# Storing dK and dV from ACT's queue in one transfer of 2 MB, instead of from GpSimd's in two

## The chip, the cores and the metric

One core of a Trainium2 chip. The time is the device time in microseconds (us) of one execution of the whole kernel; the kernel before took 701.58 us, the median of three runs (698.41 to 702.56). Engines: PE is TensorE, DVE is VectorE, ACT is ScalarE, POOL is GpSimd, SP is SyncE. Transfers (DMAs) between HBM and the core's SBUF are issued by an engine's queue and then carried out by 16 channels (DMA engines), which all queues share.

## What is computed

The backward pass of an attention with grouped heads (32 query heads, 4 key/value heads, 4 query positions, 2048 keys, 128 features, 32 batches, bfloat16), with the forward output as well:

```python
B, Hq, Hkv, Sq, Sk, D = 32, 32, 4, 4, 2048, 128
def _fwd_reference(q, k, v):
    k = jnp.repeat(k, rep, axis=1)
    v = jnp.repeat(v, rep, axis=1)
    scores = jnp.einsum("bhqd,bhkd->bhqk", q, k) * D ** -0.5
    p = _softmax(scores, axis=-1)
    return jnp.einsum("bhqk,bhkd->bhqd", p, v)
_out, _vjp = jax.vjp(_f, q, k, v)
return (out, *vjp(grad_out))        # O, dQ, dK, dV
```

K, V, dK and dV are 2.1 MB each for one batch; Q, dO, O and dQ are 32 KB each.

## The kernel before

One batch is one unit of work. The 32 query rows of each of the four K/V heads stand side by side on 128 partitions (`G` = 32 rows a head). For each batch the steps are, by their names in the kernel:

- `LK`, `LV` (lines 145 to 160): four loads of 512 KB each for K and for V, one a head, issued by SP. K has 3 buffers, V has 2. A load waits until its buffer's last reader is done: dQ for K, O for V. `LK` of the next batch but one also brings, every fourth batch, Q and dO of four batches (`GROUP`, line 137; POOL issues it).
- `QDT`, `KT0..7`, `VT0..7` (lines 167 to 190): PE turns Q, dO, K and V by multiplying with the identity matrix, DVE copies the result from PSUM to SBUF.
- `Sa`, `Sb` (line 206): scores on PE, row maximum on DVE (`negb`). `EXa`, `EXb` (line 215): Exp on ACT.
- `NRM` (line 234): 1/sum on DVE (`rinv`), then POOL makes `dop` = dO/sum and `qp` = scaled Q/sum, four instructions each (line 231). PE needs `dop` for dV and `qp` for dK.
- `ET`, `O` (lines 253, 270): E turned, the output O, and delta; POOL stores O. `dPa`, `dPb` (line 334): the gradient `ds` of the scores. `dST`, `dQ` (lines 256, 284): `ds` turned, and dQ; POOL stores dQ.
- `dV0..7`, `dK0..7` (lines 328 to 332, by `outer`, line 292): eight outer products each. PE writes two PSUM banks, and ACT casts them (line 307, 128 x 1024 elements) into a 2 MB tile in SBUF. There are 4 such tiles for dV and dK together (`out_pool`), so the tile of a batch's dK is that of dK two batches earlier, and its first cast waits until the earlier store has landed. After the eighth cast the tile is stored: `left` counts them (lines 314 to 326). The last batch is stored in four halves instead, by POOL (line 319), as they become ready.

PSUM has 8 banks, handed out by a small planner in the program (`Banks`) by age; PE waits when the bank that it was given has not yet been read by ACT or DVE.

The order of the work is written out by hand: `HEAD` for the first batches, `STEADY`, which is repeated, and `TAIL`. The instructions of each engine stand in its queue in that order, and each engine works its queue in order. In `STEADY` (`-` is the batch before, `+` the one after, `+2` the one after that) the places that matter are:

```python
dSTa- VT4 EXa VT0 QDT+ dSTb- KT4+ dK1- dK6- KT6+ KT2+ KT0+ NRM dK0- dQ- dK3- dK5- dK2- ETb ETa VT7 KT3+ VT6 VT1
dV7 dK4- O dV5 dPb dV1 KT5+ KT1+ dV3 dV6 dPa KT7+ dV2 LK+2 LV+2 VT2+ dV4 Sa+ dV0 Sb+ dK7 VT5+ VT3+ EXb+
```

`dK4-` is the eighth dK of its batch and `dV0` the eighth dV, so dK's store is issued behind `dK4-` and dV's behind `dV0`. Behind them stand, for ACT, the casts of `dV5` and of `dK7`, and the Exps.

Of the kernel before, what the change touches and what calls it, by code (L numbers as in the profile page):

```python
# [81 lines left out]
def kernel(ctx: ExitStack, tc: tile.TileContext, q, k, v, grad_out, out_0, out_1, out_2, out_3):  # L82
    nc = tc.nc
# [48 lines left out]
    store = nc.gpsimd  # L132
# [159 lines left out]
    def outer(S, x, y, dst, name, i, b, copy):  # L292

        if name not in S:
            S[name + "left"] = 8
            S[name] = out_pool.tile([P, NH, C, D], BF16, name=name, tag="outp")
        t = banks.take(2)
        ps = banks.ap(t).rearrange("p a (j c d) -> p a j c d", j=2, c=2)
        for c in range(2):
            u = P * ((2 * i + c) % 8)  # L300
            for a in range(2):
                r = slice(2 * G * a, 2 * G * a + 2 * G)
                nc.tensor.matmul(  # L303
                    ps[:, a, :, c, :], lhsT=S[f"{x}{i // 4}"][r, u:u + P], rhs=S[y][r, :, :],
                    start=True, stop=True, tile_position=(2 * G * a, 0),
                )
        copy(  # L307
            out=S[name][:, :, 2 * i:2 * i + 2, :].rearrange("p h c d -> p h (c d)"),
            in_=banks.ap(t).rearrange("p a (j w) -> p (a j) w", j=2),
        )  # L310
        banks.give(t)
        S[name + "left"] -= 1
        if b == B - 1:

            half = f"{name}half{i // 4}"
            S[half] = S.get(half, 4) - 1
            if S[half] == 0:
                c = slice(8 * (i // 4), 8 * (i // 4) + 8)
                store.dma_start(
                    out=dst[b].rearrange("p h (c d) -> p h c d", d=D)[:, :, c, :].rearrange("p h c d -> p h (c d)"),  # L320
                    in_=S[name][:, :, c, :].rearrange("p h c d -> p h (c d)"),
                )
        elif S[name + "left"] == 0:
            o = S.pop(name)
            for a in range(2):
                store.dma_start(out=dst[b][:, 2 * a:2 * a + 2, :], in_=o[:, 2 * a:2 * a + 2].rearrange("p h c d -> p h (c d)"))  # L326

    def dV(b, i, copy=nc.scalar.copy):
        outer(st[b], "e", "dop", dv_v, "dv", i, b, copy)

    def dK(b, i, copy=nc.scalar.copy):
        outer(st[b], "ds", "qp", dk_v, "dk", i, b, copy)
# [29 lines left out]
    with tc.manual_schedule():  # L362

        for w in HEAD.split():
            w, b = w.split("@")
# [5 lines left out]
        for w in TAIL.split():  # L371
            w, b = w.split("@")
# [31 lines left out]
```

## The time and the profile before

| | us |
|---|---|
| median of three runs | 701.58 (698.41 to 702.56) |
| the profiled execution | 698.71 |
| its span, first to last instruction | 696.7 |
| PE busy / ACT busy / DVE busy / POOL busy | 626.0 / 569.1 / 584.5 / 302.7 |
| moved by transfers | 274.44 MB, mean 394 GB/s |

The profile is of one execution. A page gives the busy time of each engine, the span in 40 slices (busy share in tenths; GB/s is what the transfers moved in the slice), the costliest groups of instructions and the DMA issues with the median time from issue to landing. A row of the list of waits reads "engine line waited for: us in total, times, longest us": `ACT dk L307 <- DMA out_dram<-dk: 7.1, 8, 1.8` is ACT idle before the cast at line 307 until a store of dK had landed, eight times, 7.1 us in all. A row of a timeline reads start, length, engine, line and operation, output and input, count, and in brackets the idle time before it and what ended it; instructions of one kind in a row are merged. "issue" is the call that puts a transfer into a queue; its length is not that of the transfer.

### The profile page before, as it was taken

The numbers are of one execution on the slowest core, as the hardware profiler recorded it, in microseconds if no ns is written. First come the engines' busy times: TensorE is split into PE (matmuls) and PEld (weight loads), VectorE is DVE, ScalarE is ACT, GpSimd is POOL, SyncE is SP. The second block draws the span as 40 slices with busy tenths as digits, with TensorE's granted clock in tenths as the row PEclk, the third lists the DMA queues.
The fourth block names the chain that finished last, engine by engine and source line by source line (L and its number), as shares of the span: only waits on it lengthen the run. The fifth ranks groups of instructions, "written<-read, shape, count | busy, mean of one in ns | idle before, by whom it ended". The sixth has DMA issues, their size and how long they took to land.

```text
span 696.7 us, 28064 instructions
## 1 busy us (share of the span) xinstructions
PE 626.0 (90%) x12352; PEld 454.1 (65%) x12352; DVE 584.5 (84%) x992; ACT 569.1 (82%) x673; POOL 302.7 (43%) x506
## 2 busy tenths in 40 slices
PE   5899999999998989979999798998998889998982
PEld 4577776677676656666666676667766677666661
DVE  5999999999997998869988688888988869898960
ACT  0698989899887989869888687887888868888994
POOL 1355443555454435443354424544434543345452
PEclk9999999999999999999999899999999989999997
DMA  9989999999999999999999999999999999999767
GB/s 339 400 317 411 417 415 416 416 413 415 417 415 417 414 417 416 417 409 412 415 415 413 373 397 398 400 410 382 416 416 417 415 340 393 415 414 415 289 257 274
DMA packets 75577, 274.44 MB, mean 394 GB/s; under 512 B 8448, under 2 KB 8448, under 8 KB 75456
## 3 DMA queue, kind: packets, MB, share of 16 engines
q0 software_dynamic: 37536, 138.16, 49.3%
q1 hardware_dynamic: 37920, 134.50, 48.9%
q8 instruction: 96, 1.57, 0.8%
q14 instruction: 25, 0.20, 0.1%
HBM read 136.31 MB, written 136.31 MB: 391 GB/s over the span
## 4 chain that ended last, share of the span: by engine, by line
PE 43%; DMA 33%; ACT 6%; DVE 5%; POOL 5%; issue 5%; SPq 0%; POOLq 0%; DVEq 0%; ACTq 0%
PE banks L181 18%; DMA k_sb<-in_k_dram 15%; DMA out_dram<-dk 12%; PE banks L303 10%; PE banks L264 7%; ACT dv L307 5%; PE banks L248 5%; DMA out_dram<-dv 4%; PE banks L198 3%; POOL dop L231 2%; DMA v_sb<-in_v_dram 2%; DVE kt L183 2%; DVE ds L338 1%; ACT dk L307 1%; POOL qp L231 1%
## 5 line engine op out<-in xcount | busy, mean ns | idle before, releaser
L307 ACT CAST dv<-banks 128x1024 bf16<-128x1024 f32 x256 | 245.5, 1028 | 56.9 <-PE banks L303 56.3
L307 ACT CAST dk<-banks 128x1024 bf16<-128x1024 f32 x256 | 250.7, 1025 | 34.5 <-PE banks L303 23.6
L183 DVE COPY kt<-banks 128x1024 bf16<-128x1024 bf16 x256 | 164.3, 680 | 8.3 <-PE banks L181 8.3
L183 DVE COPY vt<-banks 128x1024 bf16<-128x1024 bf16 x256 | 166.2, 680 | 1.3 <-PE banks L181 0.9
L181 PE MATMUL banks<-ident,k_sb 128*128 128x128 bf16 x2048 | 145.8, 221 | 13.1 <-DMA k_sb<-in_k_dram 8.6
L181 PE MATMUL banks<-ident,v_sb 128*128 128x128 bf16 x2048 | 143.5, 220 | 14.3 <-ACT dv L307 9.7
L231 POOL TENSOR_SCALAR dop<-do_sb,rinv 32x128 bf16<-32x128 bf16 x128 | 76.7, 599 | 181.3 <-PE banks L303 118.9
L181 PEld LDWEIGHTS <-k_sb 128*128 128x128 bf16 x2048 | 120.8, 99 | 41.9 <-issue 31.7
L181 PEld LDWEIGHTS <-v_sb 128*128 128x128 bf16 x2048 | 122.2, 98 | 28.7 <-issue 23.3
L303 PE MATMUL banks<-dop,e 64*128 64x256 bf16 x1024 | 99.3, 276 | 15.1 <-POOL dop L231 11.3
L326 POOL DMA_DIRECT2D out_dram<-dv x62 | 43.7, 709 | 138.0 <-ACT dv L307 67.6
L338 DVE SCALAR_TENSOR_TENSOR ds<-banks,delta,e 128x1024 bf16<-128x1024 f32 x64 | 82.2, 1284 | 17.3 <-PE banks L198 14.3
L303 PE MATMUL banks<-qp,ds 64*128 64x256 bf16 x1024 | 86.4, 272 | 2.1 <-ACT dk L307 1.4
L231 POOL TENSOR_SCALAR qp<-q_sb,srinv 32x128 bf16<-32x128 bf16 x128 | 78.1, 610 | 10.7
L222 ACT ACTIVATE e<-banks,negb 128x1024 bf16<-128x1024 f32 x64 | 70.7, 1111 | 8.6 <-DVE negb L214 8.5
L211 DVE TENSOR_REDUCE m<-banks 128x1 f32<-128x1024 f32 x64 | 75.1, 1215 | 0.9 <-PE banks L198 0.9
L303 PEld LDWEIGHTS <-e 64*128 64x128 bf16 x1024 | 34.0, 94 | 63.1 <-issue 46.7
L250 DVE COPY et<-banks 128x1024 bf16<-128x1024 bf16 x64 | 41.3, 686 | 29.6 <-PE banks L248 29.6
L303 PEld LDWEIGHTS <-ds 64*128 64x128 bf16 x1024 | 42.2, 94 | 28.8 <-ACT dv L307 13.1
L326 POOL DMA_DIRECT2D out_dram<-dk x62 | 44.0, 713 | 13.6 <-DMA out_dram<-dk 13.0
L250 DVE COPY dst<-banks 128x1024 bf16<-128x1024 bf16 x64 | 43.5, 681 | 5.5 <-PE banks L248 3.6
L248 PE MATMUL banks<-ident,ds 128*128 128x128 bf16 x512 | 39.4, 221 | 7.1 <-ACT dk L307 6.8
(39 smaller groups left out, 484.1 us busy)
## 6 DMA issues: line engine op xcount, KB each, us to landing
k_sb<-in_k_dram SPq DMA_DIRECT2D x128, 512.0 KB, 13.8
v_sb<-in_v_dram SPq DMA_DIRECT2D x128, 512.0 KB, 18.6
out_dram<-dv POOLq DMA_DIRECT2D x64, 1024.0 KB, 23.6
out_dram<-dk POOLq DMA_DIRECT2D x64, 1024.0 KB, 22.1
out_dram<-o_sb POOLq DMA_DIRECT2D x32, 32.0 KB, 23.2
out_dram<-dq_sb POOLq DMA_DIRECT2D x32, 32.0 KB, 16.2
q_sb<-in_q_dram POOLq DMA_DIRECT2D x7, 128.0 KB, 21.9
do_sb<-in_grad_out_dram POOLq DMA_DIRECT2D x7, 128.0 KB, 22.0
```

Of the source, the lines that this page charges most:

```text
L181: nc.tensor.transpose(out=ps[:, 4 * hh + j, :], in_=S[which][:, 2 * (i % 2) + hh, 4 * (i // 2) + j, :], identity=ident[:])
L183: nc.vector.tensor_copy(out=S[f"{which}t{i}"][:], in_=ps)
L211: nc.vector.reduce_max(out=S["m"][:, i:i + 1], in_=S[f"s{i}"][1], axis=AX.X)
L222: nc.scalar.activation(out=S[f"e{i}"][:], in_=ps, func=ACT.Exp, bias=S["negb"][:], scale=scale, accum_out=S["l"][:, i:i + 1],)
L231: nc.gpsimd.tensor_scalar(out=t[r, h % 2, :], in0=src[r, :], scalar1=by[r, :], scalar2=None, op0=ALU.mult)
L248: nc.tensor.transpose(out=ps[:, u, :], in_=S[f"{src}{i}"][:, P * u:P * u + P], identity=ident[:])
L250: nc.vector.tensor_copy(out=S[f"{name}{i}"][:], in_=ps)
L264: nc.tensor.matmul(ps[G * h:G * h + G, :], lhsT=S[f"{xt}{c // 8}"][:, c % 8, G * h:G * h + G], rhs=S[kv][:, h, c, :], start=(c == 0), stop ...
L303: nc.tensor.matmul(ps[:, a, :, c, :], lhsT=S[f"{x}{i // 4}"][r, u:u + P], rhs=S[y][r, :, :], start=True, stop=True, tile_position=(2 * G * ...
L307: copy(out=S[name][:, :, 2 * i:2 * i + 2, :].rearrange("p h c d -> p h (c d)"), in_=banks.ap(t).rearrange("p a (j w) -> p (a j) w", j=2),)
L326: store.dma_start(out=dst[b][:, 2 * a:2 * a + 2, :], in_=o[:, 2 * a:2 * a + 2].rearrange("p h c d -> p h (c d)"))
L338: nc.vector.scalar_tensor_tensor(out=S[f"ds{i}"][:], in0=ps, scalar=S["delta"][:], in1=S[f"e{i}"][:], op0=ALU.subtract, op1=ALU.mult,)
```

## The change

The tile's store after the eighth cast is one call on ACT's queue for all four heads, 2 MB, where it was two calls on POOL's queue for two heads each, 1 MB. The change holds for dK and dV of all batches but the last, whose four halves POOL still stores. `store` is `nc.gpsimd`.

```diff
         elif S[name + "left"] == 0:
             o = S.pop(name)
-            for a in range(2):
-                store.dma_start(out=dst[b][:, 2 * a:2 * a + 2, :], in_=o[:, 2 * a:2 * a + 2].rearrange("p h c d -> p h (c d)"))
+            nc.scalar.dma_start(out=dst[b], in_=o[:].rearrange("p h c d -> p h (c d)"))
```

## The prediction

> **What bounds the kernel now.** I read the page first (busy rows, slices, transfers), then the list of waits, then the timelines of the queues.
>
> ```profile
> span 696.7 us, 28064 instructions
> ...
> PE 626.0 (90%) x12352; PEld 454.1 (65%) x12352; DVE 584.5 (84%) x992; ACT 569.1 (82%) x673; POOL 302.7 (43%) x506
> ...
> GB/s 339 400 317 411 417 415 416 416 413 415 417 415 417 414 417 416 417 409 412 415 415 413 373 397 398 400 410 382 416 416 417 415 340 393 415 414 415 289 257 274
> ...
> k_sb<-in_k_dram SPq DMA_DIRECT2D x128, 512.0 KB, 13.8
> ...
> out_dram<-dv POOLq DMA_DIRECT2D x64, 1024.0 KB, 23.6
> out_dram<-dk POOLq DMA_DIRECT2D x64, 1024.0 KB, 22.1
> ```
>
> Away from the head and the last three slices, the channels move about 416 GB/s: saturated. One batch is 8.39 MB of K, V, dK and dV and some 0.13 MB of Q, dO, O and dQ, so 8.52 MB, which at 416 GB/s is 20.5 us: the channels' beat. The compute's own beat I read off SP's timeline, where the first K load of a batch starts at 40.90, 178.36 and 628.41 us, after 0, 7 and 28 batches:
>
> ```profile
> 40.90:178.36 137.46, 134.23 (x2704) 97.98 (x2702) 127.30 (x218) 124.15 (x148) 66.34 (x109) 1.00 1.01 405
> 178.36:628.41 450.05, 411.88 (x8108) 297.73 (x8106) 384.13 (x653) 373.47 (x441) 197.47 (x325) 0.98 1.02 406
> ```
>
> (Stretch, length, then busy time of PE, weight loads, DVE, ACT and POOL.) The first seven batches take 19.64 us each, with PE busy 98% and no wait for a transfer on it: compute runs faster than the channels, whose backlog grows. dK's first half lands 10.8 us after its issue at 47.9 and 22.6 us after at 247.4. The other 21 take 21.43 us: the 20.5 of the channels and some 0.9 of stops. Over all 28: 587.51 / 28 = 20.98.
>
> ```profile
> POOL out_dram L326 <- DMA out_dram<-dk: 35.1, 10, 4.4
> POOL out_dram L326 <- DMA out_dram<-dv: 22.1, 6, 4.2
> ...
> PE banks L303 <- POOL dop L231: 11.3, 11, 2.4
> ...
> ACT dk L307 <- DMA out_dram<-dk: 7.1, 8, 1.8
> ...
> PE banks L248 <- ACT dk L307: 6.8, 8, 1.8
> ```
>
> Rows one and two: POOL stands before a store until an older store has landed. Behind it in POOL's queue is dop, which PE needs (row three), as at 393:
>
> ```profile
> 393.42 0.72 POOL L326 DMA_DIRECT2D out_dram<-dv  x1 [4.11 <-DVE kt L183]
> ...
> 394.23 2.63 POOL L231 TENSOR_SCALAR dop<-do_sb,rinv 32x128 bf16<-32x128 bf16 x4
> ...
> 395.55 0.27 PE L303 MATMUL banks<-dop,e 64*128 64x256 bf16 x1 [2.43 <-POOL dop L231]
> ```
>
> rinv was ready at 389.78, dop began at 394.23, PE lost 2.43 and then 1.10 us, and that batch took 26.1 us. The last two wait rows matter most: eight times ACT stood before dK7's cast, 7.1 us in all, and PE stood right behind it for 6.8. What ACT loses at that place, PE loses in full.
>
> ```profile
> 143.23 1.01 ACT L307 CAST dv<-banks 128x1024 bf16<-128x1024 f32 x1 [0.70 <-PE banks L303]
> 144.14 1.02 ACT L307 CAST dk<-banks 128x1024 bf16<-128x1024 f32 x1
> 145.04 6.69 ACT L307 CAST dv<-banks 128x1024 bf16<-128x1024 f32 x7
> 151.62 1.03 ACT L307 CAST dk<-banks 128x1024 bf16<-128x1024 f32 x1
> ```
>
> In an undisturbed batch ACT works from dV7 (143.23) through dK4 (144.14), the other seven dV and dK7 without a gap. The new instructions go exactly here: dK's store between 144.14 and 145.04, dV's between 145.04's seven and 151.62.
>
> **The change, part by part.**
>
> *Taken from POOL:* 124 issues of 0.71 us (62 of dV, 62 of dK), 2.8 us a batch on an engine 43% busy, and with them the 57.2 us of waits above. Only where POOL made dop late did it reach the path: PE's 11.3 us, and the batches at 304, 389 and 564 (23.5, 26.1, 23.0 us). This is part of the 0.9 us of stops in the later batches. O, dQ and the Q/dO loads stay with POOL; they no longer queue behind stores, and nothing waits for their landing soon.
>
> *Put on ACT:* 62 issues, two a batch. ACT is in order, so each costs (a) the drain: the store must see the last cast finished. POOL's row: casts end at 112.21, issue at 112.51, 0.30 us; at least the 0.09 us from negb's end to the Exp. (b) The issue. No store or load leaves ACT today. SP's loads take 0.33 (alone), 0.47 (median for K) and up to 1.46 us; four times the runs do not make it longer, since the first q_sb and do_sb loads, with 512 runs, took 0.43 and 0.50. I take 0.47, because the store falls among SP's own V issues; ends 0.33 and 1.46. (c) The restart, 0.05 (the space between SP's issues), and the lost overlap of two casts, 1.02 alone against 0.945 apart in a row: 0.08. Sum 0.90 us a store; low end 0.09 + 0.33 + 0.05 + 0.08 = 0.55, high end 0.30 + 1.46 + 0.13 = 1.9.
>
> *How much reaches PE:* behind dV's store stands dK7's cast, then Exp; the 7.1 to 6.8 row says all of it: 0.90. Behind dK's store stand dV5 to dV0, whose banks PE needs. ACT has 0 to 0.43 us of idle time in that run of casts (none at 143, 0.16 + 0.27 at 125 and 127), so between 0.47 and 0.90: 0.68. Compute's beat becomes 19.64 + 0.68 + 0.90 = 21.22 us. That is above the channels' 20.5, so the backlog does not build and the waits for transfers go. 28 batches: 28 x (21.22 - 20.98) = +6.7 us.
>
> *Tail and head:* after 628.41 five stores are ACT's, and ACT is busy 54.12 of 68.3 us there and over 90% from 650 to 680: three of dK at 0.68 and two of dV at 0.90, 3.8 us, less the 1.07 us that ACT now waits for a landing at 642.67: +2.8. The last batch's four halves stay on POOL. In the head (ACT busy 25.67 of the first 50 us) one dV store: +0.3.
>
> *One transfer for two, another queue:* the same 4 KB runs on the same channels. Loads alone, 512 KB each, moved 413 GB/s from 8 to 20 us, loads and 1 MB stores together 415 to 417: no rate to gain, zero. The Trainium skill (DMA: Bandwidth & Descriptors, Rules for kernel authors) asks for 1 MiB or more in a DMA for full bandwidth; by it the 512 KB loads should run below the stores' rate, and by its 436 GB/s ceiling the beat could fall to an estimated 19.5 us. The trace does not agree, with 413 for 512 KB.
>
> *Moved past SP:* every load now waits for the landing of the load eight before it (the trace's waits of SP's queue: V's issues stand 72.3 us in 46 waits for earlier V loads). If ACT's stores join that count of eight, a batch has ten, and V's fourth load waits for dK's store, dV's store for the batch's first K load. Without backlog K lands within about 4 to 10 us (3.5 to 7.2 at 41 us) and dV's store is ready 12.5 us after K's issue: no wait. V's last load would leave, as an estimate from the 10.8 us of the early dK landing, some 18 us after K's first, and is used 33 after it (KT and VT on PE's timeline). Cost zero, as long as no backlog stands; the priced rival is below.
>
> Sum: +6.7 + 2.8 + 0.3 = +9.8 on the profiled execution's 698.71 (span 696.7 and 2.0 around it) = 708.5. Its time lies 2.9 below the median of the runs shown, 701.58; on the median the forecast is 711.
>
> **The rivals.**
>
> *The channels keep the beat (faster).* If the two stops reach PE with less than 20.5 - 19.64 = 0.86 us together, the beat is 20.5 and POOL's stops are pure gain: 28 x (20.5 - 20.98) = -13.4, tail +1.4: 690. The point is 0.43 us a stop; for it speaks the 0.55 low end with ACT's 0.43 us of slack, against it ACT's unbroken run at 143 to 152. The chance is 0.17.
>
> *Nothing moves.* The gain in POOL's stops and ACT's losses cancel within a few us, about 702: stops of 0.7 to 0.85 us. The Trainium skill (DMA: Bandwidth & Descriptors, Issuing engines are not separate DMA queues) says that another issuing engine only shifts the sequencer's issue time, usually small beside the DMA itself; that rule expects this case, and the saturated 416 GB/s agrees with its first half. Chance 0.17.
>
> *A dear issue.* SP's longest issues, 0.7 to 1.46 us, 31 of 256, came under a loaded ring. If a 2 MB store always met that: 1.9 us a store, a beat of 19.64 + 1.7 + 1.9 = 23.2, +63 and +7 in the tail, 772; half of it 740. Chance 0.12.
>
> *ACT waits for a load.* With a backlog as now, K's first load lands 14.6 us after issue, dV's store is ready at 12.8: 1.8 us of ACT in some 20 batches, +36 on the 711, 747. It needs the shared count and the backlog at once. Chance 0.09.
>
> That the change does not do what it says I see no room for: one call of 2 MB each, in ACT's program order.
>
> **How the numbers follow.** The forecast has 0.45, 711 us, by itself 703 to 722. The range must take in the faster rival and half of the dear ones: 690 to 748. One per cent, about what a measurement of this kernel can tell from no change, is 694.6 to 708.6: faster 0.15 (the first rival, nearly whole), same 0.30 (the second, and the forecast's low end), slower 0.55.
>
> **What would show it.** ACT's timeline has, twice a batch, a gap of about 0.9 us between the casts around the store, and the list of waits has PE behind ACT's dk and dv casts for some 1.6 us a batch in place of 0.3. SP's K loads come 21.2 us apart from first to last; the GB/s row stands near 402, below 416; POOL's waits for landings and PE's for dop are gone; a store lands in under 20 us throughout. If the row stays at 415 and the beat at 20.5, the stops were hidden and I am wrong; if the stops are over 1.3 us, the issue was mis-sized.

## The result, and the profile after

The changed kernel takes 707.08 us (median of seven runs, 705.49 to 708.73), the kernel before 701.58 beside it (698.41 to 702.56): a ratio of 1.0083, 95% interval 1.0061 to 1.0104. The profiled execution of after is the one of 707.08, its span 705.2; that of before was 698.71 with 696.7. So 8.5 us of span are to be found.

The page of after, the lines that answer to those shown of before:

```profile
span 705.2 us, 27947 instructions
...
PE 624.9 (89%) x12352; PEld 457.5 (65%) x12352; DVE 586.6 (83%) x992; ACT 568.9 (81%) x673; POOL 216.4 (31%) x382
...
GB/s 338 396 309 415 416 415 416 414 415 376 407 399 415 415 362 413 410 414 413 364 409 415 410 415 365 408 403 363 378 408 411 406 410 416 415 409 400 315 222 265
...
out_dram<-dv ACTq DMA_DIRECT2D x31, 2048.0 KB, 17.3
out_dram<-dk ACTq DMA_DIRECT2D x31, 2048.0 KB, 14.8
```

POOL is relieved (302.7 to 216.4 us) and stores land earlier (17.3 us for dV, where the halves took 23.6). But the GB/s row, steady in before as far as its 22nd slice, now drops to 360 to 380 every five slices or so from the tenth on. The stretches between the first K loads of the same batches as in the prediction (first seven batches, other 21):

```profile
41.57:188.54 146.97, 134.83 (x2704) 99.62 (x2702) 128.11 (x217) 124.00 (x148) 46.90 (x81) 0.99 1.01 400
188.54:636.70 448.16, 408.93 (x8108) 298.52 (x8107) 384.84 (x651) 373.12 (x442) 139.11 (x241) 0.98 1.01 402
```

Head +0.7 us (41.57 against 40.90), first seven batches +9.5 (146.97 against 137.46), other 21 batches -1.9, tail +0.2 (705.2 - 636.70 = 68.5 against 68.3). All 28 batches: 595.13 / 28 = 21.25 us, where before had 20.98.

The list of waits (who, line, for what: us in total, times, longest):

```profile
PE banks L248 <- ACT dk L307: 26.1, 31, 3.2
...
ACT dk L307 <- DMA k_sb<-in_k_dram: 12.4, 5, 3.3
...
PE banks L303 <- POOL dop L231: 1.3, 2, 1.1
```

POOL's waits for landings are gone, and PE's wait for `dop` fell from 11.3 to 1.3 us. PE's wait behind ACT's dK casts rose from 6.8 us in 8 times to 26.1 in 31: what ACT loses there reaches PE. New is the second row: ACT, which casts, stands for a *load* of K. ACT's timeline shows what a store costs it, first in a quiet batch:

```profile
127.35 1.02 ACT L307 CAST dk<-banks 128x1024 bf16<-128x1024 f32 x1
128.39 0.38 ACTq L325 DMA_DIRECT2D out_dram<-dk  x1
128.87 6.51 ACT L307 CAST dv<-banks 128x1024 bf16<-128x1024 f32 x7 [0.51 <-PE banks L303]
```

and in one that was not quiet:

```profile
329.75 0.38 ACTq L325 DMA_DIRECT2D out_dram<-dv  x1
330.23 1.01 ACT L307 CAST dk<-banks 128x1024 bf16<-128x1024 f32 x1 [2.63 <-DMA k_sb<-in_k_dram]
```

The quiet store takes ACT 0.50 us from cast to cast (128.37 to 128.87), and a quiet batch 20.25 us. In the other the store itself was held back by some 2.1 us: it was issued when the second K load of its own batch had landed. There are ten transfers a batch on SP's and ACT's queues (four of K, dK, four of V, dV), and each waits for the landing of the one eight before it; for dV that is K's second load. It happens at 159.7, 245.1, 330.2, 415.8 and 629.8 us. PE stands for 3.21, 2.37, 2.60, 2.10 and 1.93 us at those places, the first four are followed by 3.4 us of half the granted clock, and the batches around the first four last 24.6, 23.8, 24.0 and 24.3 us. A fifth long one, 25.2 us at 465, has another cause: PE stood 2.29 us at 473.7 for nothing that the list of waits shows (it comes up again below).

Why does a 512 KB load take 12 to 14 us to land when nearly all of it is there after 8 to 10? Its count is raised sixteen times in the trace, which I take as once by each channel. The times of these sixteen arrivals after the issue, in us, sorted:

```
K load, before, 41 us    2.9 3.0 3.0 3.1 3.1 3.1 3.1 3.1 3.1 3.1 3.1 3.2 3.2 3.3 3.3  3.5
K load, before, 304 us   3.9 4.0 4.1 4.5 5.3 5.7 6.6 6.6 6.8 7.2 7.2 7.6 7.7 8.0 8.0 14.3
dV half, before, 623 us  9.1 9.2 9.2 9.3 9.4 9.7 9.9 9.9 9.9 10.0 10.8 10.9 11.2 11.2 11.2 30.5
K load, after, 315 us    4.9 4.9 5.2 5.3 5.6 5.6 5.8 5.9 6.1 6.1 6.2 6.4 6.5 6.5 7.3 12.2
```

In the first row, early in the run, all sixteen come together. In the others fifteen come within 2 to 4 us of each other and one is late, in both kernels, by 5 to 19 us. A mean of 416 GB/s hides that.

### The profile page after: what moved, and what is told of

It is laid out like the page before. It is cut to its first block, busy times and chain, and to the rows that moved or that the text cites. A ratio compares the mean times of both kernels' runs of the same rounds, so it can differ in the third digit from the quotient of the medians.

```text
span 705.2 us, 27947 instructions
## 1 busy us (share of the span) xinstructions
PE 624.9 (89%) x12352; PEld 457.5 (65%) x12352; DVE 586.6 (83%) x992; ACT 568.9 (81%) x673; POOL 216.4 (31%) x382
## 3 DMA queue, kind: packets, MB, share of 16 engines
q0 software_dynamic: 3808, 8.13, 3.2%
q8 instruction: 96, 1.57, 0.8%
## 4 chain that ended last, share of the span: by engine, by line
PE 50%; ACT 22%; DMA 15%; issue 6%; DVE 2%; ACTq 2%; POOL 2%; SPq 0%; POOLq 0%; DVEq 0%
PE banks L181 20%; ACT dv L307 17%; DMA k_sb<-in_k_dram 15%; PE banks L303 12%; PE banks L248 8%; PE banks L264 8%; ACT dk L307 4%; PE banks L198 2%; ACTq L325 2%; DVE kt L183 1%; POOL dop L231 1%; PE banks L171 1%; DVE vt L183 0%; DVE ds L337 0%; POOL qp L231 0%
## 5 line engine op out<-in xcount | busy, mean ns | idle before, releaser
L307 ACT CAST dv<-banks 128x1024 bf16<-128x1024 f32 x256 | 242.3, 1033 | 51.9 <-PE banks L303 50.3
L181 PEld LDWEIGHTS <-k_sb 128*128 128x128 bf16 x2048 | 121.3, 100 | 35.1 <-issue 32.2
L181 PEld LDWEIGHTS <-v_sb 128*128 128x128 bf16 x2048 | 123.9, 99 | 26.1 <-issue 20.0
L303 PE MATMUL banks<-dop,e 64*128 64x256 bf16 x1024 | 97.7, 275 | 9.6 <-issue 3.8
L303 PE MATMUL banks<-qp,ds 64*128 64x256 bf16 x1024 | 84.7, 273 | 1.3 <-ACT dk L307 1.0
L303 PEld LDWEIGHTS <-e 64*128 64x128 bf16 x1024 | 35.5, 94 | 55.7 <-issue 37.7
L248 PE MATMUL banks<-ident,ds 128*128 128x128 bf16 x512 | 41.4, 227 | 26.2 <-ACT dk L307 26.1
L303 PEld LDWEIGHTS <-ds 64*128 64x128 bf16 x1024 | 40.1, 94 | 28.6 <-ACT dv L307 12.7
L250 DVE COPY dst<-banks 128x1024 bf16<-128x1024 bf16 x64 | 43.8, 685 | 14.5 <-PE banks L248 14.4
L248 PEld LDWEIGHTS <-ds 128*128 128x128 bf16 x512 | 34.8, 102 | 30.3 <-issue 30.3
L198 PE MATMUL banks<-vt,qdt 128*32 128x512 bf16 x512 | 40.5, 387 | 5.9 <-ACT dv L307 5.9
## 6 DMA issues: line engine op xcount, KB each, us to landing
out_dram<-dv ACTq DMA_DIRECT2D x31, 2048.0 KB, 17.3
```

The source lines that it names most:

```text
L181: nc.tensor.transpose(out=ps[:, 4 * hh + j, :], in_=S[which][:, 2 * (i % 2) + hh, 4 * (i // 2) + j, :], identity=ident[:])
L198: nc.tensor.matmul(ps[G * h:G * h + G, a, :], lhsT=S["qdt"][:, col, G * h:G * h + G], rhs=xt[:, 4 * (h % 2):4 * (h % 2) + 4, :].rearrange( ...
L248: nc.tensor.transpose(out=ps[:, u, :], in_=S[f"{src}{i}"][:, P * u:P * u + P], identity=ident[:])
L250: nc.vector.tensor_copy(out=S[f"{name}{i}"][:], in_=ps)
L303: nc.tensor.matmul(ps[:, a, :, c, :], lhsT=S[f"{x}{i // 4}"][r, u:u + P], rhs=S[y][r, :, :], start=True, stop=True, tile_position=(2 * G * ...
L307: copy(out=S[name][:, :, 2 * i:2 * i + 2, :].rearrange("p h c d -> p h (c d)"), in_=banks.ap(t).rearrange("p a (j w) -> p (a j) w", j=2),)
```

## The experiments

**First four.** Theory 1: ACT's wait for K is the loss, and with the waits on ACT and on POOL both gone the channels' 20.5 us show. Theory 2: ACT's stops at the stores, or PE's waits for K, keep the time where it is. `act_k_two` is after, and `before_k_two` before, with K in two calls; `pool_one` leaves the store on POOL but in one call; `act_dk_only` moves dK alone and leaves dV's two halves on POOL.

```diff
-        for h in range(NH):
-            nc.sync.dma_start(out=S["k"][:, h].rearrange("p c d -> p (c d)"), in_=k_v[b, h])
+        for h in range(0, NH, 2):
+            nc.sync.dma_start(out=S["k"][:, h:h + 2].rearrange("p h c d -> p h (c d)"), in_=k_v[b, h:h + 2].rearrange("h p x -> p h x"))
```
```diff
+            store.dma_start(out=dst[b], in_=o[:].rearrange("p h c d -> p h (c d)"))     # pool_one
...
+            if name == "dk":                                                            # act_dk_only
+                nc.scalar.dma_start(out=dst[b], in_=o[:].rearrange("p h c d -> p h (c d)"))
```

> The changed kernel, but K is loaded in two calls of 1 MB instead of four of 512 KB. Loads by SP and stores by ACT share eight completion counts in turn, and a transfer waits for the landing of the one eight before it; with ten a batch dV's store waits for the second K load of the same batch, with eight a batch for the dV store of the batch before, which landed long ago. Theory 1 (the loss of the changed kernel is ACT's stop of some 0.6 us a store, of which 0.75 us a batch reach PE, and on top the waits of dV's store for a K load in about six batches): the batches of 24 us go, all batches take 20.3 to 20.6, 28 x (21.25 - 20.5) = 21 us less than the changed kernel, 684 to 690. Theory 2 (the waits only take the place of waits for the channels, and the two stops alone make the loss): 703 to 709, the mean batch stays near 21.2. Theory 3 (fewer, larger loads arrive later and PE waits for K): over 709.

> The kernel before, with K in two calls of 1 MB: the control for the K loads alone, stores by POOL as before. Theory 1 and 2: the size of the K loads is nothing in itself; within 1% of before, 697 to 707, with POOL's waits before its stores still there. If the K loads themselves gain, this falls to 690 or less, and the gain of the kernel with ACT's stores and two K calls is not that of the counts.

> The kernel before with one store of 2 MB for dK and for dV, still on POOL's queue: the other half of the change. POOL then issues 4 transfers a batch in place of 6 (and Q and dO every fourth batch), its eight completion counts reach back nearly two batches, and it should no longer stand before a store. Theory 1: the stops of POOL that made dop late go, no stop on ACT comes; the beat of the channels is left, 28 x 20.5, 10 to 14 us less than before: 688 to 692. Rival: POOL's stops were only a way for the channels' backlog to show, and another wait takes their place (the dK tile still being stored, loads of K): within 1% of before, 697 to 706.

> Only dK's store goes to ACT in one transfer of 2 MB, dV's stays with POOL in two of 1 MB. Then no store of ACT waits for a K load of the same batch (dK's, eight back, for a V load of the batch before). Theory 1: one stop of 0.6 us a batch on ACT, compute's beat about 20.0 at most, below the channels' 20.5; POOL has four transfers a batch and no longer stands: 689 to 694. Theory 2 (every stop on ACT adds to the time, the waits do not matter): half of the loss of the changed kernel, about 704.

| kernel | us | ratio to before (95%) | 28 batches, us each |
|---|---|---|---|
| before | 700.50 | | 20.98 |
| act_k_two | 703.20 | 1.0038 (1.0023 to 1.0052) | 21.08 |
| before_k_two | 701.25 | 1.0003 (0.9990 to 1.0017) | 21.07 |
| pool_one | 701.86 | 1.0019 (1.0005 to 1.0032) | 21.09 |
| act_dk_only | 706.85 | 1.0087 (1.0058 to 1.0115) | 21.23 |

Theory 1 fell in all three: no kernel came near 690. With K in two calls a batch has eight transfers, so each waits for its counterpart of the batch before; ACT's wait for K is gone, and less than half of the loss stays. With one call on POOL its stops are gone, and nothing is gained. In both PE now waits for K itself, in act_k_two

```profile
PE banks L181 <- DMA k_sb<-in_k_dram: 15.5, 13, 2.9
```

and in pool_one

```profile
PE banks L181 <- DMA k_sb<-in_k_dram: 25.6, 19, 2.3
```

In act_dk_only that wait is 29.5 us. There ACT waits for no load at all, and yet the whole of after's loss is there (1.0087 against 1.0083), more than either theory gave. Take one wait away and another takes its place: something behind them all sets the pace, and the late channel is the candidate.

**Next four.** Theory A: that channel needs about 21.1 us for a batch whatever the queue, so the last 21 batches are alike in every variant and the loss sits in the first seven. Theory B: ACT loses time at every store, all along.

```diff
-            nc.scalar.dma_start(out=dst[b], in_=o[:].rearrange("p h c d -> p h (c d)"))
+            if b >= 8:                       # act_late;  act_early: if b < 8
+                nc.scalar.dma_start(out=dst[b], in_=o[:].rearrange("p h c d -> p h (c d)"))
+            else:
+                for a in range(2):
+                    store.dma_start(out=dst[b][:, 2 * a:2 * a + 2, :], in_=o[:, 2 * a:2 * a + 2].rearrange("p h c d -> p h (c d)"))
```
```diff
             o = S.pop(name)                  # before_stop
+            for n in range(2):
+                nc.scalar.copy(out=stop[:], in_=stop[:])
```

> Stores of batches 0 to 7 leave as in the kernel before (GpSimd, two of 1 MB), all later ones as in the kernel after. Theory A (one channel of the sixteen needs about 21.1 us for a batch whatever the queue, so from about the eighth batch on no variant can go faster, and the loss of after lies in the first seven batches, 147.0 against 137.5 us): the first seven take 137 to 139 us, the other 21 take 447 to 451, and the time is that of before, ratio 0.996 to 1.003. Theory B (ACT loses time at every store, and the loss of 0.83% is spread over the run): three quarters of the loss stay, ratio 1.005 to 1.008.

> The other half: stores of batches 0 to 7 leave as in the kernel after (ACT, 2 MB), all later ones as in the kernel before. Theory A: the whole loss stays, the first seven batches take 143 to 147 us, the other 21 take 447 to 451, ratio 1.005 to 1.012. Theory B: a quarter of the loss, ratio 1.000 to 1.004.

> The kernel before, with its stores on GpSimd, and at the place of each store two copies of 128x64 on ACT, one behind the other, which take ACT some 0.5 to 0.7 us as the store did in the kernel after (an addition to the work, nothing is left out). It has ACT's stops without the move to another queue. Theory A: the first seven batches take 141 to 144 us, the other 21 stay at 447 to 452, ratio 1.004 to 1.010. Theory B: 28 batches lose 0.75 us each on top of GpSimd's stops, +15 to +21 us, ratio 1.02 to 1.03.

> Transfers only, all computation left out: K and V are loaded as in the kernel (four of 512 KB each) and stored straight back as dK and dV from the same buffers, in one 2 MB transfer each on ACT's queue; Q and dO go to O and dQ on GpSimd's queue. Theory A (a slow channel, there whatever the engines do): the batches are 21.0 to 21.4 us apart, and of the sixteen arrivals of a transfer one comes 3 us or more behind the others. Rival (the lag comes from the work beside the transfers, such as the fetch of TensorE's instructions): the batches are 20.5 us apart or less, and the sixteen arrivals lie within 3 us.

| kernel | us | ratio to before (95%) | first seven / other 21 batches, us | 28 batches, us each |
|---|---|---|---|---|
| before | 700.91 | | 137.5 / 450.1 | 20.98 |
| act_late | 709.45 | 1.0132 (1.0112 to 1.0152) | 138.6 / 455.5 | 21.22 |
| act_early | 698.94 | 0.9971 (0.9958 to 0.9984) | 146.9 / 439.7 | 20.95 |
| before_stop | 700.45 | 1.0005 (0.9989 to 1.0022) | 139.7 / 448.6 | 21.01 |
| copy_act | 658.0 (one run) | | | 20.06 |

Theory B falls: in before_stop two copies take ACT 0.53 and 0.58 us at the two places, the early batches stretch from 19.5 to 19.9 us, and the time stays where it was. (The stop costs ACT some 0.45 us, three quarters of what after's costs; it is not the full size.) Theory A falls as I put it, too: act_late, act_early and before_stop all came out outside the ranges of both theories. act_early lost all of the first seven batches' 9.5 us and gained it back: with little backlog at the 190th microsecond, its other 21 batches took 439.7. It beats both kernels, by 0.29% of before. act_late had before's fast start and then paid in one place. ACT's timeline there:

```profile
205.24 1.02 ACT L307 CAST dk<-banks 128x1024 bf16<-128x1024 f32 x1
210.89 0.38 ACTq L326 DMA_DIRECT2D out_dram<-dk  x1
211.37 3.76 ACT L307 CAST dv<-banks 128x1024 bf16<-128x1024 f32 x4 [5.11 <-DMA v_sb<-in_v_dram]
...
223.12 0.38 ACTq L326 DMA_DIRECT2D out_dram<-dv  x1
223.61 1.01 ACT L307 CAST dk<-banks 128x1024 bf16<-128x1024 f32 x1 [3.77 <-DMA k_sb<-in_k_dram]
```

In the batches ahead, POOL's stores had let a backlog grow (dV's halves landed 28 us after issue, K's first load 20). The first store that ACT issues into it, dV's at 192.63, goes out at once; the next two wait 5.11 us for a V load and 3.77 for a K load, and this batch takes 32.1 us. That is the wait of after, with a larger backlog: where both stores move, the dearest thing about the move is that ACT's stores wait in one count with the loads, so that a late channel stops the engine that casts.

copy_act says whose lateness it is not. Transfers alone, on the same queues, run at 20.06 us a batch, 420 to 421 GB/s, and the sixteen arrivals stay together (at 259 us: 13.4 to 13.8; at 443: 11.0 to 12.5; the last is nowhere more than 1.5 us behind the fifteenth). The late channel is not made by the transfers alone. Besides the engines' work and the queue of the stores, its page differs from that of before in one row. copy_act:

```profile
q1 hardware_dynamic: 36864, 134.23, 50.3%
q10 hardware_dynamic: 33792, 134.22, 49.8%
q0 software_dynamic: 2816, 4.20, 1.8%
q14 instruction: 5, 0.03, 0.0%
```

before (packets, MB, share of the sixteen engines' span):

```profile
q8 instruction: 96, 1.57, 0.8%
```

PE has 12352 matmuls and as many weight loads; 1.57 MB is some 64 bytes for each of them, in 96 packets of 16 KB.

**Last four.** Theory C: the loss of after is ACT's wait for K. Theory D: that wait only shows the late channel, and another would take its place. To tell them apart K stays in four calls and V goes in two (the same edit in the V loop), which also makes eight transfers a batch. And the copies get PE instructions beside them:

```diff
+        for n in range(386):                 # copy_act_pe; copy_act_pe2: 772, of 32 columns
+            nc.tensor.matmul(banks[:, :128], lhsT=ident[:], rhs=ident[:], start=True, stop=True)
```

> The kernel after, with V loaded in two transfers of 1 MB in place of four of 512 KB. A batch then has eight transfers on SP's and ACT's queues (four of K, dK, two of V, dV), so each waits for its own counterpart of the batch before and dV's store no longer for a K load of its own batch; K stays in four. Theory C (the loss of after is ACT's wait for a K load that one late channel holds back, every fourth batch): ACT has no wait for K, no batch over 23 us from this cause, and the time is 697 to 702, ratio 0.995 to 1.003. Theory D (ACT's wait only shows the late channel, and without it another wait, PE's for K, takes the same time): 703 to 708, ratio 1.003 to 1.010.

> Control: the kernel before with V in two transfers of 1 MB. Theory C and D: no change, ratio 0.998 to 1.002.

> The transfers alone as in copy_act, all computation left out, and beside them 386 matmuls with 386 weight loads a batch on TensorE, whose result nobody reads and which wait for nothing: as many TensorE instructions as the real kernel has. If the fetch of instructions takes one channel, a row of some 1.5 MB of instruction transfers is there, one of the sixteen arrivals of a transfer lies 2 us or more behind the others, and the batches are 20.5 to 22 us apart in place of 20.0. If the late channel comes from something else (the data of the engines, SBUF traffic), the sixteen arrivals stay within 2 us and the batches at 20.0.

> As copy_act_pe, with twice the instructions, 772 matmuls of 32 columns and 772 weight loads a batch. Instruction fetch: what the batches lost in copy_act_pe against 20.0 us doubles, and the instruction row shows some 3 MB. Something else: 20.0 us.

| kernel | us | ratio to before (95%) | 28 batches, us each |
|---|---|---|---|
| before | 699.81 | | 20.98 |
| act_v_two | 703.51 | 1.0057 (1.0040 to 1.0075) | 21.10 |
| before_v_two | 701.94 | 1.0036 (1.0020 to 1.0051) | 21.04 |
| copy_act_pe | 696.7 (one run) | | 20.93 |
| copy_act_pe2 | 975.8 (one run) | | 21.06 |

copy_act_pe is the find of the study: with as many PE instructions as the kernel has, which wait for nothing and touch no transferred data, the transfers go from 20.06 to 20.93 us a batch, the rate from 421 to some 408 GB/s, and the last arrival falls behind again (of a dK store at 267 us 14.5 against 11.3 for the fifteenth, of a K load at 460 us 13.0 against 8.2). The whole time of 696.7 us is that of PE itself, which is busy 99% of the span. copy_act and copy_act_pe are one run each, on two chips; before takes 700.91 us beside the one and 699.81 beside the other, 0.2% apart, where the step is 4%. The instruction row is back:

```profile
q8 instruction: 96, 1.57, 0.8%
```

In the trace of copy_act_pe such a packet lasts some 0.95 us, and while one lasts 15.3 data packets are in flight on average, 16.3 otherwise: one channel of the sixteen stands for it. That does not explain the whole loss. Three packets a batch, if always on the same channel, would hold it up by an estimated 2.8 us, and 0.87 was lost; and the data packets of 4 KB themselves last longer, 163.9 ns on average from 300 to 600 us, where copy_act has 159.0.

In copy_act_pe2 the loss did not double, because PE could not be fed twice as fast. Its timeline:

```profile
201.50 3.51 PE L128 MATMUL banks<-ident 128*128 128x32 bf16 x128 [2.35 <-issue]
207.70 3.57 PE L128 MATMUL banks<-ident 128*128 128x32 bf16 x128 [2.69 <-issue]
212.80 3.56 PE L128 MATMUL banks<-ident 128*128 128x32 bf16 x128 [1.52 <-issue]
```

128 matmuls with their weight loads are 256 instructions, 16 KB, one packet; then PE stands, waiting for nothing that the list of waits shows. It goes on 1.2 to 1.6 us behind the end of an instruction packet at each of its 79 stands of over 1 us between 100 and 600 us. The fifth long batch of after holds a stand of this kind:

```profile
475.97 0.58 PE L303 MATMUL banks<-dop,e 64*128 64x256 bf16 x3 [2.29 <-issue]
```

Here an instruction packet ends at 474.47, 1.49 us before PE goes on. So what PE lacked in that batch was, by all signs, its instructions. Back in copy_act_pe2, two stretches of the same run, while the transfers last and after them (PE busy, count; weight loads; POOL; clock; DMA share; GB/s):

```profile
100.00:600.00 500.00, 295.78 (x10713) 288.84 (x10710) 0.00 (x0) 0.64 1.02 405
700.00:950.00 250.00, 229.97 (x8787) 224.42 (x8784) 0.00 (x0) 1.00 0.02 4
```

21.4 matmuls a us under load, 35.1 without. The granted clock differs as well, 0.64 and 1.00, yet a matmul keeps PE busy 27.6 ns in the first stretch and 26.2 in the second; the difference lies in the stands. The kernel needs 386 in 21.0 us, 18.4 a us: not far below what the loaded channels bring. Per microsecond copy_act_pe2 fetched 20% more than copy_act_pe (21.4 against 8959 / 500 = 17.9) and lost 1.00 us a batch against 0.87, so it speaks for the fetch, though the doubling that I expected was not to be had and a difference of 0.13 us rests on one run each.

act_v_two has no wait of ACT for K, one stretch of half clock ahead of its tail (at 225 us) where after has five, and one batch over 23 us (23.9). Its 703.51 us still lies in theory D's range: of after's 0.83% 0.57 stay; its own control lost 0.36 (why, is open), so against the control 703.51 / 701.94 = 1.0022, as act_k_two against its control, 1.0028. Both theories hold a part: without ACT's wait for K, against these controls, two thirds of the loss or somewhat more are gone, and what is left shows as PE's wait for K, here

```profile
PE banks L181 <- DMA k_sb<-in_k_dram: 18.1, 20, 2.0
```

**What stands.** Shown, by one run each: the stream of PE's instructions beside the transfers takes the channels from 20.06 to 20.93 us a batch, with one arrival of sixteen late, and each instruction packet stops one channel while it lasts. Shown in repeated runs: before was at that pace already (20.98), so there was little to gain by taking work from POOL (0.29% in act_early was the most); stops of ACT of three quarters of the size, beside POOL's stores, cost nothing; after's long batches are, but for one, those where ACT waits for a load.

Argued, not shown: that the late arrival is the channel that carries the instructions (the trace does not number the channels, and the estimate of 2.8 us speaks against its being always the same one); that ACT's wait for K is the cause of after's loss, since act_dk_only loses as much without it; that the half clock behind ACT's waits, and the emptied channels (371 to 385 GB/s in the batch behind each of the first four), are why the time is not regained; what the last 0.2 to 0.3% is. One candidate is the depth of the backlog: at the last K load a dV store in before was still 24.7 us from landing, in after 8.5, and what is late there is moved in the tail, which is no longer for it (68.3 and 68.5 us). Open, too, is a gap between the copies and the kernel: the last 21 batches of copy_act take 19.95 us each, those of copy_act_pe 20.79, and the undisturbed batches of before 21.1.

## Why the prediction was right or wrong

The time came out near the forecast, 707.08 for 711, and so did the beat, 21.25 for 21.22. The way there did not.

- *"The channels' beat", 20.5 us:* the step that failed. 8.52 MB at the mean 416 GB/s is the pace only as long as all sixteen channels keep up. What is waited for is the last of sixteen arrivals, and the pace with PE's instructions beside the transfers is 20.93 (copy_act_pe). The first K loads of before stand 21.0 to 21.2 us apart in its undisturbed batches from 199 to 304 us, where compute alone had shown 19.6; that could have told me.
- *The stop, 0.90 us a store:* mis-sized. Drain 0.02 for 0.30, issue 0.38 for 0.47, restart 0.10 for 0.05; with the lost overlap of 0.08 it is 0.58, at the low end of 0.55. The 2 MB issue never took longer, so the dear issue is out.
- *"How much reaches PE", 1.58 us a batch:* 0.75, from 19.5 to 20.25 in quiet batches.
- *"That is above the channels' 20.5, so the backlog does not build":* 20.25 lies below 20.93, so it built, and what I had made the condition of the fourth rival was there.
- *28 x 0.24 = +6.7:* measured +7.6, but not as 56 stops: before_stop shows that stops of three quarters of the size, alone, are worth 0.05%, with zero inside the interval. The long batches stand at five waits; that these are the cause is argued, since act_dk_only loses as much without them.
- *"Cost zero, as long as no backlog stands" and the rival "ACT waits for a load", 0.09:* this took place, five times instead of in some 20 batches, as it seems because each wait empties the channels and the backlog needs about four batches to come back. With 1.98 to 3.25 us for each, the usual 0.50 included, its price was near the 1.8.
- *POOL's stops as gain:* gone, as said, but worth nothing to the end: pool_one has none and takes 0.19% longer.
- *Head +0.3, tail +2.8:* +0.7 and +0.2. That ACT's stops met idle time in the tail was not tried by itself.
- *"The channels keep the beat", 690:* its condition, stops under 0.86 us a batch together, was met (0.75), and there was no gain, because the beat that the channels keep is not 20.5.
- *"Nothing moves":* the Trainium skill's rule that I set beside it (DMA: Bandwidth & Descriptors, Issuing engines are not separate DMA queues) holds for the issue, 0.38 us; the wait for an older transfer's landing, which came with the new queue, is a cost that it leaves out.

Two errors cancelled: a stop that was too dear, and a channel pace that was too fast. That the number came out is luck. The forecast of the profile tells them apart: 0.9 us gaps, a steady 402 GB/s and evenly spaced K loads were not there; dips at every fourth batch were.

## What to carry to other kernels

Before moving a transfer to a queue of an engine on the path, list which older transfers it must wait for: here one count of eight held stores and loads together, and the engine that casts stood for a load it has nothing to do with. Read a saturated channel by the last of a transfer's arrivals and by the spacing of loads, not by mean GB/s; and when three variants trade one wait for another at the same time, look for the resource behind the waits, with the transfers alone as a kernel of their own.

## What the runs showed of the hardware

- A PE that executes 17.9 matmul and weight-load pairs a us beside saturated transfers costs them 4% (20.06 to 20.93 us a batch, copy_act and copy_act_pe); its instructions are 1.57 MB, 0.6% of the bytes. While one of their packets of 16 KB lasts, some 0.95 us, one channel of sixteen stands (15.3 data packets in flight for 16.3).
- Under saturated transfers PE was supplied with 21.4 such pairs a us, without them it ran 35.1 (copy_act_pe2). It went on 1.2 to 1.6 us behind the end of an instruction packet.
- One arrival of sixteen lags, in the loads of after as in those of before; after's own dK stores do not (median 0.4 us). The Trainium skill (DMA: Bandwidth & Descriptors, Latency and other measured facts) says that two of the channels are usually slower and guesses at the descriptor rings of GpSimd's queue. The traces do not agree with that guess: the lag is there in after with 8.13 MB on that queue, at most 1.5 us in copy_act with 4.20 MB, and back in copy_act_pe with the same 4.20 MB and PE's instructions.
- In after the granted clock fell to half for 3.4 us behind PE stops of 2.10 to 3.21 us, and not behind one of 1.93. The length of the stop alone does not decide: pool_one kept the full clock behind a stop of 2.13 us at 220.7.
